# Moving a batch's loads behind another couple of a fused attention and max-out kernel, with four output buffers instead of three

## The chip, the cores and the metric

The kernel runs on one core of a Trainium2 chip. The metric is device time in microseconds (us), the median of several runs. The engines are TensorE (PE: matmuls, with its weight loads shown as PEld), VectorE (DVE), ScalarE (ACT), GpSimd (POOL) and SyncE (SP). PE multiplies into PSUM, DVE and ACT carry results from PSUM to SBUF, and POOL and SP do here little else than issue DMAs: POOL the loads from and the stores to memory (the software queue of the profile), SP the transposing DMAs from SBUF to SBUF (the hardware queue). Both queues feed the same 16 DMA engines.

## The reference

There are 8 batches of 3072 rows. For each batch a square score matrix is made from z alone, rectified and squared; it multiplies v, and the result is gated by u. All rows then go through a max-out layer.

```python
scores = (1.0 / S) * np.matmul(z, z.transpose(0, 2, 1))   # 8 x 3072 x 3072
attn = np.maximum(scores, 0.0) ** 2
x = u * np.matmul(attn, v)                                 # 8 x 3072 x 256
h1, h2 = x @ w1, x @ w2                                    # 24576 x 1024
out = np.maximum(h1, h2) @ w_out                           # 24576 x 256
```

The kernel uses that max(h1, h2) = relu(x(w1 - w2)) + x w2, so it keeps w1 - w2 and the product w2 w_out.

## The kernel before, in words

A batch has 24 tiles of 128 rows. Four tiles make a group (six to a batch), two groups make a couple (three to a batch); a couple is the unit of the main loop. The score matrix is cut into 6 by 6 blocks of 512 by 512. It is symmetric, so only the blocks on and above the diagonal are computed (`score_pair`: two matmuls into PSUM, line 204; a rectifying copy by ACT, line 217; squaring by DVE, lines 223 and 225). The blocks below the diagonal are mirrored by a transposing DMA on SP (`mirror`, line 246), and a diagonal block, of which only a triangle is computed in batches 1 to 7, is completed by three small transposes (line 228). Pairs of a coming couple or batch are computed between the steps of the present couple.

Batch 0 is special. Its groups 0 to 3 (couples (0,0) and (0,1)) are run as plain products, group by group, in the loop over `PLAIN` (line 262). Its last couple, (0,2), is run in the main loop as 96 steps of plain products over the blocks 2, 0, 1, 3, 5, 4 (line 835); in these steps 20 of the score pairs of batch 1 are computed, at steps 2, 6, 11, 16, 20 and on, up to 91. A pair needs the transposed z (tile `zT`) of the pieces it touches: piece 1 of batch 1 first at step 20, piece 2 first at step 58. From batch 1 on, each couple is computed with seven products of combined blocks instead of eight (`prepare`, the sums and differences S1 to S4 of blocks by DVE, line 300; of v by `combine_v`, lines 164 to 167).

The two matmuls of a step run in the two halves of PE's rows. Where a product passes from one half to the other, a `nop` on POOL stands between them (lines 844 to 849): POOL waits for the last matmul of the first half, and PE's first matmul in the second half waits for POOL. In couple (0,2) such a pair of relays stands every fourth step, and whatever is in POOL's queue ahead of a relay delays it.

The feed-forward part of a couple (`ff`, lines 435 to 476) runs one couple later: the 16 inner products `d_ps` go through ACT into the tiles `g_sb`, three ahead of their use, and the output of each group leaves in two halves (`leave`): ACT copies a PSUM bank into an `o_sb` buffer (line 475) and POOL issues the store (line 476). So a couple has four such copies, two after its first group and two at its end. `opool` has three buffers, so the fourth copy waits until the first store has landed. Couple (0,0)'s part runs between the plain groups and couple (0,2); the bank of its fourth copy is needed by the first step of couple (0,2).

The instructions stand in each engine's queue in the order in which the program calls them, and each queue is served in order. A load that has no buffer to wait for is issued as soon as POOL reaches it; `held=True` writes one element with DVE first, which makes the load wait for that DVE instruction.

Loads around the change: `load_v(1, 2)` at group 3, tile 18 (line 685, held), `load_u` for couple (0,2) in `loads_behind(1)` (line 710) and `load_v(1, 1)` just after (line 743) come before the feed-forward part of (0,0); each `load_v` is four DMAs of two tiles (128 KB). `load_v(1, 0)` comes in `loads_behind(2)`, at the end of couple (0,2). `turn_u` (line 180) transposes u on SP: for couple (0,2) at its steps 2 and 6 (line 813); the result is read by `gate` after the couple's last step. v of batch 1 is first read by `combine_v`, after couple (0,2).

Of the kernel before, what the change touches and what calls it, by code (L numbers as in the profile page):

```python
# [11 lines left out]
def kernel(  # L12
# [43 lines left out]
    rpool = ctx.enter_context(tc.tile_pool(name="rpool", bufs=3))  # L56
    hpool = ctx.enter_context(tc.tile_pool(name="hpool", bufs=5))
    xpool = ctx.enter_context(tc.tile_pool(name="xpool", bufs=4))
    gpool = ctx.enter_context(tc.tile_pool(name="gpool", bufs=8))
    opool = ctx.enter_context(tc.tile_pool(name="opool", bufs=3))  # L60
    mm_psum = ctx.enter_context(tc.tile_pool(name="mm_psum", bufs=4, space=bass.MemoryType.PSUM))
    acc_psum = ctx.enter_context(tc.tile_pool(name="acc_psum", bufs=1, space=bass.MemoryType.PSUM))

    def by_tile(x):
        return x.rearrange("(p t) d -> p t d", t=NT)
# [76 lines left out]
    def load_v(b, piece, lo=0, n=2 * G, held=False):  # L142
        if (b, piece) not in vp:
            vp[b, piece] = vpool.tile([P, 2 * G, D], bf16, name="v_sb")
        t = vp[b, piece]
        if held:
            nc.vector.memset(t[:, lo, 0:1], 0.0)
        step = 2 if b else n
        for at in range(lo, lo + n, step):
            nc.gpsimd.dma_start(  # L150
                out=t[:, ds(at, step), :], in_=by_tile(v[b])[:, ds(piece * 2 * G + at, step), :]
            )
# [21 lines left out]
    def load_u(b, g):  # L174
        un[b, g] = unat.tile([P, G, D], bf16, name="un")
        nc.gpsimd.dma_start(out=un[b, g], in_=by_tile(u[b])[:, ds(g * G, G), :])  # L176

    def turn_u(b, g):
        t = upool.tile([P, G, KD, P], bf16, name="uT")
        nc.sync.dma_start_transpose(  # L180
            t.rearrange("p a c r -> p (a c) r"), un[b, g].rearrange("p a d -> p (a d)")
        )
        uT[b, g] = t
# [318 lines left out]
    couples = [(b, c) for b in range(B) for c in range(NC)]  # L502
# [44 lines left out]
    def steps_of(i):  # L547
        tiles, both = range(NT), range(KD)
        head = edge(i - 1) if i else 0
        tail = NT - edge(i)  # L550
        steps = [(n, dc) for dc in both for n in tiles[:head]]
        steps += [(n, dc) for n in tiles[head:tail] for dc in both]
        return steps + [(n, dc) for dc in both for n in tiles[tail:]]

    def pair_slots(i):
        return (
            [1, 3] + list(range(6, 40, 4)),
            list(range(3, 41, 4)),
            list(range(3, 41, 4)),
            list(range(0, 44, 4)),  # L560
        )[i]

    def need(b, g, n):
        most = pair_at[b, g, 2 * g]
        for t in range(n + 1):
            if t // G >= g:
                most = max(most, pair_at[b, g, t // 2] + 1)
        return most

    with tc.manual_schedule():  # L570
# [17 lines left out]
        def new_acc():  # L588
            return {
                (half, dc): acc_tile(2 * half + dc) for half in range(2) for dc in range(KD)  # L590
            }
# [27 lines left out]
        for i in range(PLAIN):  # L619
            b, g = groups[i]  # L620
            if i:
                acc = new_acc()
            new, slots = {}, pair_slots(i)
            for slot, (n, dc) in enumerate(steps_of(i)):
                k = need(b, g, n)
                upto = max(k, min(done + 1, k + AHEAD)) if slot in slots else k
                while done < min(upto, len(pairs)):
                    emit_pair()
                if i == 0 and slot in (10, 22):
                    zT_pe(12 if slot == 10 else 20, 8 if slot == 10 else 4, "act")  # L630
                    if slot == 22:
                        for x in z_first:
                            x.release()
                attn_unit(b, g, n, acc, dc, n == 0, n == NT - 1)
                if n == NT - 1 and i < PLAIN - 1:
                    if i < 2:
                        new[dc] = drain_fast(acc, dc)
                    else:
                        new.update(drain(acc, [dc]))
                if dc:  # L640
                    continue
                if i in (1, 2) and n == 10:
                    for h in sums.values():
                        nc.vector.tensor_add(h[0], h[0], h[1])
                    sums = {k: h[0] for k, h in sums.items()}
                if i and n == 12:
                    xTs[groups[i - 1]], tasks = gate(*groups[i - 1], sums)
                    for task in tasks:
                        task()
                if i == 0 and n == 14:  # L650
                    turn_u(0, 0)
                if i + 1 < PLAIN:
                    if i and n == 1:
                        load_u(*groups[i + 1])
                    if n == (13 if i == 2 else 16):
                        turn_u(*groups[i + 1])
                if (i, n) in ((0, 20), (1, 10)):
                    w_in = ((w2_sb, moe_w2), (w1_sb, moe_w1)) if i == 0 else ((w_out_sb, moe_w_out),)
                    nc.vector.memset(w_in[0][0][:, 0, 0:1], 0.0)
                    for w_sb, w in w_in:  # L660
                        nc.gpsimd.dma_start(
                            out=w_sb, in_=w.rearrange("(c p) f -> p c f", p=P)
                        )
                if later and n % 4 == 0 and (i == 3 or i and n > 12):
                    later.sort(key=lambda block: (block[2] > 3, block[1], block[2]))
                    mirror(*later.pop(0))
                if i == 2 and n == 16:
                    nc.vector.tensor_sub(w15_sb, w1_sb, w2_sb)
                    w1.release()
                    for dc in range(KD):  # L670
                        tp = mm_psum.tile([P, KF, P], bf16, name="tpw", tag="mm")
                        for j in range(KF):
                            nc.tensor.transpose(
                                tp[:, j, :], w2_sb[:, dc, ts(j, P)], ident
                            )
                        nc.scalar.copy(w2T_sb[:, dc, :, :], tp)
                    w2.release()
                if (i, n) in ((1, 16), (2, 14)):
                    load_z(1, i - 1, held=True)
                if (i, n) in ((2, 8), (3, 10)):  # L680
                    turn_z(1, i - 2)
                if (i, n) == (3, 14):
                    load_z(1, 2, held=True)
                if (i, n) == (3, 18):
                    load_v(1, 2, held=True)
            if i == 2:
                for dc in range(KD):
                    ps = mm_psum.tile([P, D], fp32, name="w2o_ps", tag="mm")
                    for nb in range(KF):
                        nc.tensor.matmul(  # L690
                            ps,
                            w2T_sb[:, dc, nb, :],
                            w_out_sb[:, nb, :],
                            start=(nb == 0),
                            stop=(nb == KF - 1),
                        )
                    nc.scalar.copy(W2o_sb[:, dc, :], ps)
                w2T.release()
            sums = new
# [4 lines left out]
        def loads_behind(i):  # L704
            b, c = couples[i]
            if c == 2 and b + 1 < B:
                load_v(b + 1, 0)
            if i + 1 < len(couples):
                for q in range(2):
                    load_u(couples[i + 1][0], 2 * couples[i + 1][1] + q)  # L710
            if b and b + 1 < B and c < 2:
                load_z(b + 1, c + 1)
                load_v(b + 1, c + 1)
            if c == 2 and b + 2 < B:
                load_z(b + 2, 0)
# [23 lines left out]
        b, g = groups[PLAIN - 1]  # L739
        sums = drain(acc, range(KD))  # L740
        xTs[b, g], gates = gate(b, g, sums)
        loads_behind(PLAIN // 2 - 1)
        load_v(1, 1)
        forms, early, late = prepared(PLAIN // 2)
        second(PLAIN // 2 - 2, gates + [lambda: turn_z(1, 2)])

        for i in range(PLAIN // 2, len(couples)):
            b, c = couples[i]
            q1, q2 = 2 * c, 2 * c + 1
            target = min((b + 1) * per_batch + (-6, 8, 22)[c], len(pairs))  # L750
            steps, ends, marks, waits = steps_of_couple(
                b, c, forms, blocks=() if b else (2, 0, 1, 3, 5, 4)
# [37 lines left out]
            events = {}  # L790
# [19 lines left out]
                    events.setdefault(n, []).insert(0, do)  # L810
            if not b:
                events[len(steps)] = [after_plain]
            for n, do in ((2, lambda: turn_u(b, q1)), (6, lambda: turn_u(b, q2))):
                events.setdefault(n, []).append(do)
            if b and b + 1 < B:
                events.setdefault((30, 8, 8)[c], []).append(lambda: turn_z(b + 1, c))

# [78 lines left out]
```

## Time and profile before

| what | value |
|---|---|
| median of 3 runs | 933.38 us (931.15 to 936.52) |
| the profiled execution's own time | 935.3 us |
| its span | 933.4 us |
| PE busy | 908.8 us, 97% of the span |
| DVE, ACT, POOL busy | 684.2, 633.2, 140.9 us |
| hardware DMA queue (SP's transposes) | 91.14 MB, 64.0% of 16 engines' span |
| software DMA queue (POOL's loads and stores) | 53.62 MB, 30.6% |
| mean granted PE clock | 0.994 |

An engine's busy time is the union of its instructions. The view of waits says for how long an engine stood idle before a line, and which instruction ended it; the timeline lists instructions by start time, with the idle time before one in brackets, and can show SP's DMA issues (SPq), whose duration is the time that the issuing took SP. A window's row has the busy time of each engine in a stretch, the granted clock and the share of the DMA engines, which can be above 1 where transfers of two queues overlap. Stretches of couple (0,2): the plain groups end at 66.3 us, the feed-forward part of (0,0) ends at 82.0, the couple's steps end at 115.3, the feed-forward part of (0,1) ends at 131.3, where couple (1,0) begins.

### The profile page before, as it was taken

How to read it: one execution, taken by the hardware profiler on the slowest of the kernel's cores; microseconds unless marked ns; L12 is line 12 of the kernel's file. 1: busy time of each engine (PE TensorE's matmuls, PEld its weight loads, DVE VectorE, ACT ScalarE, POOL GpSimd, SP SyncE). 2: the span in 40 equal slices, each digit the busy share in tenths (PEclk: the TensorE clock that was granted, in tenths of full speed). 3: DMA queues.
4: the chain of work that ended last, by engine and by line, in shares of the span. 5: the costliest groups of instructions: out<-in, count | busy, mean ns of one | idle time of the engine just before them, and what ended most of it. 6: DMA issues, size and time to landing. Idle time of an engine off the chain costs nothing.

```text
span 933.4 us, 19582 instructions
## 1 busy us (share of the span) xinstructions
PE 908.8 (97%) x7490; PEld 530.5 (57%) x7538; DVE 684.2 (73%) x1043; ACT 633.2 (68%) x1219; POOL 140.9 (15%) x266
## 2 busy tenths in 40 slices
PE   8997999999999999999999999999999999999998
PEld 4454555664655656655556556566565564655655
DVE  6770569778787689776796868969689668795542
ACT  7794856767676777667767676766776767674543
POOL 3121111022011210220202102202021021000000
PEclk9998999999999999999999999999999999999999
DMA  9999899999998999989989899799998999986401
GB/s 186 166 195 178 135 221 154 195 113 208 168 127 176 173 164 162 166 150 187 150 151 187 136 179 182 123 190 139 173 188 126 192 139 189 160 124 128 87 24 68
DMA packets 391838, 146.01 MB, mean 156 GB/s; under 512 B 362944, under 2 KB 377664, under 8 KB 391744
## 3 DMA queue, kind: packets, MB, share of 16 engines
q1 hardware_dynamic: 359904, 91.14, 64.0%
q0 software_dynamic: 31840, 53.62, 30.6%
q8 instruction: 59, 0.97, 0.4%
q14 instruction: 35, 0.29, 0.1%
HBM read 59.77 MB, written 25.17 MB: 91 GB/s over the span
## 4 chain that ended last, share of the span: by engine, by line
PE 84%; DMA 5%; issue 5%; DVE 4%; ACT 1%; POOL 1%; ACTq 0%; DVEq 0%; POOLq 0%
PE acc L835 39%; PE acc L457 19%; PE d_ps L435 15%; PE s_ps L204 6%; PE acc L262 4%; DMA out_dram<-o_sb 3%; DVE blk L300 2%; DMA v_sb<-in_v_dram 1%; ACT r_sb L217 1%; DMA blk<-blk 1%; DVE blk L223 1%; POOL v_sb L150 0%; DVE blk L225 0%; DVE h_sb L771 0%; PE acc L597 0%
## 5 line engine op out<-in xcount | busy, mean ns | idle before, releaser
L835 PE MATMUL acc<-blk,v_sb 64*128 64x512 bf16 x2208 | 398.6, 379 | 9.3 <-ACT o_sb L475 5.8
L217 ACT ACTIVATE r_sb<-s_ps 128x512 bf16<-128x512 f32 (+3 forms) x664 | 330.3, 559 | 109.0 <-PE s_ps L204 62.5
L300 DVE TENSOR_TENSOR blk<-blk,blk 128x2048 bf16<-128x2048 bf16 x252 | 301.7, 1219 | 28.7 <-PE acc L835 15.2
L835 PE MATMUL acc<-blk,vt 64*128 64x512 bf16 x1512 | 311.9, 377 | 3.1 <-ACT o_sb L475 3.1
L448 ACT ACTIVATE g_sb<-d_ps 128x512 bf16<-128x512 f32 x376 | 217.9, 602 | 110.4 <-PE d_ps L435 89.9
L225 DVE TENSOR_TENSOR blk<-r_sb 128x1024 bf16<-128x1024 bf16 x251 | 170.2, 689 | 129.2 <-ACT r_sb L217 127.8
L835 PEld LDWEIGHTS <-v_sb 64*128 64x128 bf16 x2208 | 161.0, 95 | 132.8 <-issue 18.2
L457 PE MATMUL acc<-w_out_sb,g_sb 128*128 128x256 bf16 x1536 | 226.5, 273 | 0.0
L435 PE MATMUL d_ps<-xT,w_sb 128*128 128x512 bf16 x720 | 214.2, 379 | 2.6 <-issue 0.2
L457 PEld LDWEIGHTS <-g_sb 128*128 128x128 bf16 x1536 | 150.3, 98 | 84.0
L835 PEld LDWEIGHTS <-vt 64*128 64x128 bf16 x1512 | 123.3, 94 | 75.7 <-issue 10.0
L204 PE MATMUL s_ps<-zT 64*128 64x512 bf16 (+3 forms) x672 | 150.4, 358 | 2.1 <-DVE r_sb L215 0.5
L476 POOL DMA_DIRECT2D out_dram<-o_sb x92 | 49.9, 547 | 374.1 <-ACT o_sb L475 360.5
L435 PEld LDWEIGHTS <-w_sb 128*128 128x128 bf16 x768 | 73.3, 98 | 28.2 <-issue 9.8
L475 ACT COPY o_sb<-acc 128x512 f32<-128x512 f32 x96 | 52.3, 590 | 52.8 <-PE acc L457 31.4
L150 POOL DMA_DIRECT2D v_sb<-in_v_dram x90 | 48.5, 566 | 136.5 <-PE acc L835 105.5
L204 PEld LDWEIGHTS <-zT 64*128 64x128 bf16 x672 | 46.7, 95 | 38.7 <-issue 2.8
L223 DVE TENSOR_TENSOR blk<-r_sb 128x512 bf16<-128x512 bf16 (+3 forms) x170 | 46.2, 318 | 27.3 <-ACT r_sb L217 27.0
L771 DVE TENSOR_TENSOR h_sb<-h_sb,acc 128x512 f32<-128x512 f32 x84 | 55.3, 679 | 6.7 <-PE acc L835 6.7
L415 DVE SCALAR_TENSOR_TENSOR xT<-h_sb,uT 128x512 bf16<-128x512 f32 x96 | 59.9, 683 | 0.0
L176 POOL DMA_DIRECT2D un<-in_u_dram x48 | 26.2, 559 | 213.0 <-PE acc L835 167.1
L262 PE MATMUL acc<-blk,v_sb 64*128 64x512 bf16 x384 | 50.5, 376 | 1.9 <-DVE blk L225 1.1
(50 smaller groups left out, 274.1 us busy)
## 6 DMA issues: line engine op xcount, KB each, us to landing
out_dram<-o_sb POOLq DMA_DIRECT2D x92, 256.0 KB, 4.5
un<-in_u_dram POOLq DMA_DIRECT2D x48, 256.0 KB, 8.0
v_sb<-in_v_dram POOLq DMA_DIRECT2D x84, 128.0 KB, 8.3
blk<-blk SPq DMA_TRANSPOSE x246, 4.8
zn<-in_z_dram POOLq DMA_DIRECT2D x21, 128.0 KB, 8.5
v_sb<-in_v_dram POOLq DMA_DIRECT2D x6, 256.0 KB, 7.1
blk<-in_moe_w_dram POOLq DMA_DIRECT2D x2, 512.0 KB, 7.2
out_dram<-o_sb SPq DMA_DIRECT2D x4, 256.0 KB, 2.1
```

Source lines behind the costliest of these rows:

```text
L204: nc.tensor.matmul(s_ps[h][:, lo[h] :], zT[rows, z_at(b, blk * G + tiles[h]), :], zT[rows, q + lo[h] // P : q + G, :].rearrange("p t c -> ...
L217: nc.scalar.activation(o, s, AF.Relu)
L223: nc.vector.tensor_mul(a[:, tiles[h], lo[h] :], o, o)
L225: nc.vector.tensor_mul(a[:, k : k + 2, :], r, r)
L262: nc.tensor.matmul(a.out(acc[half, dc]), v_at(b, t, dc)[rows], a.moving(rows, j), start=first, stop=last,)
L300: op(*((by_key(x) if mixed else x.ap) for x in blocks))
L415: lambda dc=dc: nc.vector.scalar_tensor_tensor(out=x[:, dc, :].rearrange("p (t r) -> p t r", r=P), in0=hs[dc].rearrange("p (t r) -> p t r" ...
L435: nc.tensor.matmul(d_ps, w15_sb[:, kc, ts(nb, P)], xs[q][:, kc, :], start=(kc == 0), stop=(kc == KD - 1),)
L448: nc.scalar.activation(g_sb[q, nb], d_ps, AF.Relu)
L457: nc.tensor.matmul(o_ps[key][:, t % 2, :], x[:, ts(t, P)], w, start=first, stop=ends and t % 2 == 1 and n == len(weights) - 1,)
L771: nc.vector.tensor_add(out, a, b_)
L835: mm = nc.tensor.matmul(a.out(acc[name]), w()[rows], a.moving(rows, j), start=first, stop=left[name] == 0, skip_group_check=True,)
```

## The change

`load_v(1, 2)` and `load_v(1, 1)` are removed from their places, with the DVE write that held the first. In couple (0,2) eight loads of two tiles each are put at steps 12, 19, 26, 33, 40, 47, 54 and 61: the four of piece 2, then the four of piece 1. The two loads of u for couple (0,2) move from ahead of the feed-forward part of (0,0) to the couple's steps 0 and 4, and their transposes from steps 2 and 6 to 40 and 46. `opool` has four buffers, `gpool` seven.

On POOL, the four stores of (0,0) now come ahead of these ten loads, and the ten loads stand between the relays of the couple. On SP, the two transposes of u move behind the six small transposes of two diagonal blocks and the mirrors of the blocks (1,2) and (1,3) of batch 1. PE and ACT keep their order; DVE has one memset of one element less.

```diff
-    gpool = ctx.enter_context(tc.tile_pool(name="gpool", bufs=8))
-    opool = ctx.enter_context(tc.tile_pool(name="opool", bufs=3))
+    gpool = ctx.enter_context(tc.tile_pool(name="gpool", bufs=7))
+    opool = ctx.enter_context(tc.tile_pool(name="opool", bufs=4))
...
-                if (i, n) == (3, 18):
-                    load_v(1, 2, held=True)
...
-            if i + 1 < len(couples):
+            if i + 1 < len(couples) and (b, c) != (0, 1):
                 for q in range(2):
                     load_u(couples[i + 1][0], 2 * couples[i + 1][1] + q)
...
         loads_behind(PLAIN // 2 - 1)
-        load_v(1, 1)
...
-            for n, do in ((2, lambda: turn_u(b, q1)), (6, lambda: turn_u(b, q2))):
+            for n, do in (
+                (2 if b else 40, lambda: turn_u(b, q1)),
+                (6 if b else 46, lambda: turn_u(b, q2)),
+            ):
                 events.setdefault(n, []).append(do)
+            if not b:
+                events.setdefault(0, []).append(lambda: load_u(b, q1))
+                events.setdefault(4, []).append(lambda: load_u(b, q2))
+                for n in range(8):
+                    events.setdefault(12 + 7 * n, []).append(
+                        lambda n=n: load_v(1, 2 - n // 4, 2 * (n % 4), 2)
+                    )
```

## The prediction

> **What bounds the kernel.** I read the busy times first. PE fills the span, so a change can only pay where PE stands still or runs at a lower clock.
>
> ```profile
> PE 908.8 (97%) x7490; PEld 530.5 (57%) x7538; DVE 684.2 (73%) x1043; ACT 633.2 (68%) x1219; POOL 140.9 (15%) x266
> ```
>
> Next the view of waits, for PE and for the engine that PE waits on. Columns: total us, times, longest.
>
> ```profile
> ACT o_sb L475 <- DMA out_dram<-o_sb: 16.9, 7, 5.0
> ...
> PE acc L835 <- ACT o_sb L475: 8.9, 4, 5.8
> ...
> PE acc L835 <- DVE blk L300: 2.2, 2, 1.1
> ```
>
> PE's largest idle groups behind the couples' matmuls are ACT's output copy, itself often waiting for a store to land, and DVE's block sums. The timeline of PE places them; the number in brackets is the idle time.
>
> ```profile
> 82.02 0.39 PE L835 MATMUL acc<-blk,v_sb 64*128 64x512 bf16 x1
> 88.18 1.01 PE L835 MATMUL acc<-blk,v_sb 64*128 64x512 bf16 x3 [5.77 <-ACT o_sb L475]
> ...
> 135.37 0.59 PE L835 MATMUL acc<-blk,v_sb 64*128 64x512 bf16 x3 [1.07 <-DVE blk L300]
> 137.77 0.58 PE L835 MATMUL acc<-blk,v_sb 64*128 64x512 bf16 x1 [1.14 <-DVE blk L300]
> ...
> 251.20 0.37 PE L835 MATMUL acc<-blk,vt 64*128 64x512 bf16 x1 [1.29 <-ACT o_sb L475]
> ```
>
> The other two of the four stand at 474.51 (1.10) and 809.74 (0.73). The chain of waits through the first one:
>
> ```profile
> 76.16 11.28 DMA out_dram<-o_sb
> 87.54 0.59 ACT o_sb L475
> 88.18 1.01 PE acc L835 x3
> ```
>
> The first store took 11.3 us to land, against a median of 4.5 over the kernel. What it shared the DMA engines with is seen in the issues of POOL, then SP, before it:
>
> ```profile
> 65.70 2.12 POOL L150 DMA_DIRECT2D v_sb<-in_v_dram  x4 [0.91 <-DVE v_sb L147]
> 67.78 1.10 POOL L176 DMA_DIRECT2D un<-in_u_dram  x2
> 68.82 1.13 POOL L150 DMA_DIRECT2D v_sb<-in_v_dram  x2
> ```
>
> ```profile
> 61.08 4.86 SPq L246 DMA_TRANSPOSE blk<-blk  x2
> 66.03 9.33 SPq L246 DMA_TRANSPOSE blk<-blk  x1
> 75.41 10.33 SPq L246 DMA_TRANSPOSE blk<-blk  x1
> 85.84 4.78 SPq L246 DMA_TRANSPOSE blk<-blk  x1
> 90.72 1.25 SPq L134 DMA_TRANSPOSE zT<-zd  x1
> ```
>
> A mirror takes SP 2.4 us before the loads and 9 to 10 with them: loads, stores and mirrors share full engines, and SP falls behind. The windows show the price on PE's clock (PEclk, third from the right) and DMA engines that are free later:
>
> ```profile
> 86.00:90.00 4.00, 1.82 (x10) 1.03 (x11) 0.12 (x1) 1.33 (x3) 0.54 (x1) 0.54 1.21 224
> 90.00:94.00 4.00, 4.00 (x27) 2.30 (x25) 1.14 (x4) 1.34 (x5) 0.00 (x0) 0.61 1.24 283
> ...
> 106.00:110.00 4.00, 4.00 (x40) 2.03 (x38) 2.20 (x4) 3.58 (x8) 0.00 (x0) 1.00 0.24 49
> ```
>
> **The change, part by part.** All is summed against the profiled span, 933.4 us, which is the median of the runs (933.38); that execution's own time was 935.3, 1.9 above.
>
> A, the wait at 82 to 88. With four buffers the fourth copy has one of its own. ACT was idle 5.05 us before it, so it starts at 82.49, ends at 83.07, and PE restarts at 83.13 instead of 88.18. Saved: 5.05 us; 0.7 us of idle time stays, since the bank must still be copied.
>
> B, the clock behind it. The granted clock is half from 86.29 to 93.12 in the trace. PE works in 4.94 us of that (from 88.18), and does half: 2.47 us lost. With 0.7 us idle the clock has no reason to fall: the 1.29 us stop at 251 left it at 1.00. Saved: 2.47 us.
>
> C, the wait at 135 to 138. PE waits for block differences by DVE, and DVE's chain had stood 4.53 us for a mirror that SP issued at 127.63 and that landed at 134.0: SP's backlog from 66 on, carried forward. The two stops make 2.21 us, and the clock is half again from 137.49 to 140.90, 3.13 us of it worked: 1.56 us. Will the mirror come in time? Without loads the three mirrors from 66.03 take about 2.5 us each (61.08 to 66.03 held two), so the transpose of z issued at 90.72 goes at about 74 to 76, and SP is idle until DVE finishes the first diagonal block at step 12. Couple (0,2) then runs 83.1 to 107.8 (24.7 us at full clock). SP has from about 87: six small transposes at 1.28 (7.7), two mirrors, u's two transposes (3.4 before), two mirrors, then the one in question. Mirrors cost 2.5 alone and 3.7 to 7.3 in the stretch 110 to 127 before, with loads beside them; I take 4 for the first two and the 7.3 and 4.1 of before for the next two, where v's piece 0 and u fall: 87 + 7.7 + 8 + 3.4 + 11.4 = 117.5, landing 6.4 later as before: 123.9. DVE wants it at 129.57 - 7.52 = 122.05, and PE waits only if the last of DVE's three differences behind the mirror (3.7 us of work) is late for the matmul at 137.77, which without the two stops and with A and B stands at 137.77 - 2.21 - 7.52 = 128.0: the mirror may land until 124.3. Between ends: 2.5 a mirror throughout gives 114.5 for the landing and all 3.77 us saved; 10 for the first two gives 136 and a PE stop of some 12, which needs loads as dense as those of 66 to 73 (ten in 7 us), while here ten are spread over 16. The middle is nearest; I take C in full, 3.77 us, and keep 0 and worse for the range.
>
> D, the later stops. 251.20, 474.51 and 809.74 follow the same fourth copy: ACT idled 3.38 us before that at 250.56, 3.18 at 473.88, and at 809.10 the store issued at 799.95 had landed at 809.00. With a fourth buffer: 1.29 + 1.10 + 0.73 = 3.12 us. The other waits of ACT for stores (210, 361, 622, 694) held no PE stop over 0.2 us: nothing.
>
> E, the ten loads between relays. A load takes POOL 0.53 to 0.67 us (v, 90 of them). Relays come in pairs about 1.08 us apart (94.53 and 95.00, then 95.45 and 95.66, and so on); at most one load stands between two pairs and starts just after the earlier. So 0.67 fits, cost 0; no row has a load there, so the other end is ten times 0.67, 6.7 us, if nothing of it were covered. Each load also waits for the DMA eight places before it. That is a store of (0,0) for the third to sixth of v and a load of u for the last two: stores landed in 4.4 to 11.3 us, u in 11.8 to 12.6 at the worst, against 13 us from u's issue (84) to the seventh load of v (97). Cost 0, with half a microsecond in hand.
>
> [...]
>
> F, the rest. Seven tiles of g: only three are made ahead of their use, so nothing waits; eight or seven make no difference. The removed memset is 0.06 us of DVE, idle there for 20 us. u's transposes land near 107 by the sum above; the gates that read them ran after 137 (130 now): 20 us of cover. v's last part, issued at 99.8, lands by 113 at worst (13.2 in the stretch of ten loads), by 107 at its median of 8.3; DVE wants piece 1 from 109.7, so 3 us of DVE's chain are at stake in the worst case.
>
> Sum: 5.05 + 2.47 + 3.77 + 3.12 = 14.4, and 933.4 - 14.4 = 919.0.
>
> **The rivals.**
>
> 1, C does not come: the mirrors of batch 1 stay late because v's parts now run beside them. For it: SP is at 100% of its time from 35 to 140. Against it: the free engines of 102 to 110. A, B, D alone: 10.6 us, 922.8; every microsecond that the mirror lands later than before's own lag adds one, so 925 at 2 us. It decides from a landing at 124.3 on, by the sum in C only 0.4 us away.
>
> 2, the first stop is replaced. Couple (0,2) now starts 5 us earlier, and its pair at step 20 (88.2) needs the transposed z that landed at 94.2 before. If SP is not ahead, PE waits 6.0 us there, and a fall of the clock may follow: 919 + 6 to 8.5 = 925 to 927.5. It decides if the three mirrors from 66.03 take over 6.3 us each; 2.5 without loads speaks against it.
>
> 3, the DMA congestion only moves, and A, B and C all go to later waits: D alone, 930.3, same.
>
> 4, slower: POOL holds PE. Each load stands ahead of relays. If a load took POOL, or its wait, 2.5 us (1.08 of spacing plus 1.44), ten would eat the 14.4; from about 3 us on it is slower than before by the bound below: 933.4 + 5 = 938. Longest load before: 0.673.
>
> **How the numbers follow.** Half a per cent (4.7 us) is about what a measurement of this kernel can tell from no change. Chances: forecast 0.55, its own range 916.3 to 921.7 (half of the spread of the runs before, 2.7); rival 1 0.22; rival 2 0.10; rival 3 0.06; rival 4 0.07. The range goes from 916.3 to rival 2's middle, 926.5. Faster (below 928.7): 0.87; same 0.06; slower 0.07.
>
> [...]
>
> **What will show it.** A: no idle time over 1 us before the first L835 near 83, no ACT wait for stores anywhere. B and C: the granted clock at 1.00 from 5 us to the end of the work. SP's transpose of z near 75, not 90. D: no L835 stop behind L475 after batch 1. E: relays (L844) in pairs at 1.08 us with loads between. The prediction falls if PE stops in couple (0,2) behind POOL or DMA, or if DVE's chain before couple (1,0) still waits for a mirror or now for v.

## The result and the profile after

The changed kernel took 930.68 us (median of 20 runs, 919.1 to 941.92), the kernel before, timed beside it, 939.41 us (20 runs, 931.15 to 958.65). The ratio is 0.9891, with a 95% interval from 0.9856 to 0.9926; timed once more later it was 0.9928 (0.9886 to 0.9971). The ratios leave out the slow executions of both kernels, so they differ a little from the quotients of the medians (0.9907 here). So the change makes the kernel about 1% faster, where 1.54% (14.4 of 933.4 us) had been forecast, and the time is above the range. Part of the distance is the starting point: the three runs that the forecast started from (933.38) lie at the low end of what the kernel before does.

The profiled execution (934.33 us, the fourth longest of the twenty) has a span of 932.6 us, 0.8 below the one before it. Its view of waits for PE:

```profile
PE acc L842 <- DVE blk L300: 9.2, 3, 7.4
PE acc L842 <- DVE h_sb L768: 3.3, 2, 1.6
PE s_ps L204 <- DMA zT<-zd: 1.9, 2, 1.2
...
PE acc L842 <- ACT o_sb L475: 0.6, 1, 0.6
```

ACT's output copy has gone from 8.9 to 0.6 us, and DVE's block sums have grown from 2.2 to 9.2. (The couples' matmul is line 842 now, the relay 851.) The timeline of PE has both places:

```profile
82.10 0.39 PE L842 MATMUL acc<-blk,v_sb 64*128 64x512 bf16 x1
83.11 0.59 PE L842 MATMUL acc<-blk,v_sb 64*128 64x512 bf16 x3 [0.62 <-ACT o_sb L475]
...
125.80 1.02 PE L842 MATMUL acc<-blk,v_sb 64*128 64x512 bf16 x7
134.24 1.01 PE L842 MATMUL acc<-blk,v_sb 64*128 64x512 bf16 x3 [7.42 <-DVE blk L300]
```

The 5.77 us stop at 82 is 0.62 us long, as forecast. But couple (1,0), which starts some 7.5 us earlier, stands for 7.42 us at nearly the same moment as before (134.24 against 135.37). The chain of waits leads through one transfer:

```profile
111.52 21.35 DMA blk<-blk
132.87 0.03 issue
```

This is the mirror of block (1,4) of batch 1. The timelines of SP and of DVE show it from both ends:

```profile
104.48 3.10 SPq L246 DMA_TRANSPOSE blk<-blk  x1
107.69 3.72 SPq L246 DMA_TRANSPOSE blk<-blk  x1
111.52 12.49 SPq L246 DMA_TRANSPOSE blk<-blk  x1
```

```profile
119.57 0.43 DVE L165 TENSOR_TENSOR v_sb<-v_sb 128x512 bf16<-128x512 bf16 x1 [6.71 <-DMA v_sb<-in_v_dram]
...
122.30 3.61 DVE L300 TENSOR_TENSOR blk<-blk,blk 128x2048 bf16<-128x2048 bf16 x3
132.96 3.62 DVE L300 TENSOR_TENSOR blk<-blk,blk 128x2048 bf16<-128x2048 bf16 x3 [7.05 <-DMA blk<-blk]
```

In the kernel before, SP had issued the same mirror later, and DVE had waited less for it:

```profile
127.63 3.33 SPq L246 DMA_TRANSPOSE blk<-blk  x1
...
134.09 3.62 DVE L300 TENSOR_TENSOR blk<-blk,blk 128x2048 bf16<-128x2048 bf16 x3 [4.53 <-DMA blk<-blk]
```

SP now reached it at 111.52, 16 us earlier than before, but needed 12.5 us to issue it, and it landed 21.35 us after its issue began (6.4 before). Beside it stood the loads from the end of couple (0,2):

```profile
106.69 2.12 POOL L150 DMA_DIRECT2D v_sb<-in_v_dram  x4 [6.88 <-PE s_ps L204]
108.77 1.10 POOL L176 DMA_DIRECT2D un<-in_u_dram  x2
109.81 0.59 POOL L126 DMA_DIRECT2D zn<-in_z_dram  x1
```

DVE waited for both: 6.71 us for v's piece 0, then 7.05 us for the mirror. Without the second wait its sums would have gone on at 125.9 (122.30 + 3.61) instead of 132.96, so the mirror is what held PE. PE's granted clock fell to 0.50 within the stop and stayed there behind it, as the windows show (third from the right):

```profile
131.00:133.00 2.00, 0.00 (x0) 0.00 (x0) 0.04 (x1) 0.00 (x0) 0.00 (x0) 0.50 1.29 178
133.00:137.00 4.00, 2.68 (x12) 0.91 (x13) 3.97 (x4) 0.98 (x2) 0.00 (x0) 0.50 1.21 201
```

A landmark says what is gained and given back in these two executions. The feed-forward part of (0,1) begins at 107.92 instead of 115.41: 7.49 us gained. The next one, behind couple (1,0), begins at 156.24 instead of 157.37: 1.13 us are left. From there to the end it is 776.3 us against 776.1.

### The profile page after: what moved, and what is told of

Read it like the earlier page. It is cut to its first block, busy times and chain, and to the rows that moved or that the text cites. A ratio compares the mean times of both kernels' runs of the same rounds, so it can differ in the third digit from the quotient of the medians.

```text
span 932.6 us, 19607 instructions
## 1 busy us (share of the span) xinstructions
PE 906.0 (97%) x7490; PEld 524.2 (56%) x7538; DVE 684.3 (73%) x1042; ACT 634.5 (68%) x1219; POOL 140.8 (15%) x266
## 4 chain that ended last, share of the span: by engine, by line
PE 89%; DMA 5%; DVE 4%; issue 1%; ACT 1%; POOL 0%; ACTq 0%; DVEq 0%; POOLq 0%
PE acc L842 41%; PE acc L457 21%; PE d_ps L435 16%; PE s_ps L204 6%; PE acc L262 4%; DMA blk<-blk 2%; DMA v_sb<-in_v_dram 2%; DVE blk L300 2%; DMA zT<-zd 1%; DVE blk L225 1%; DVE xT L415 0%; ACT r_sb L217 0%; DVE blk L223 0%; PE w2o_ps L688 0%; POOL v_sb L150 0%
## 5 line engine op out<-in xcount | busy, mean ns | idle before, releaser
L225 DVE TENSOR_TENSOR blk<-r_sb 128x1024 bf16<-128x1024 bf16 x251 | 170.3, 690 | 129.4 <-ACT r_sb L217 128.2
L204 PE MATMUL s_ps<-zT 64*128 64x512 bf16 (+3 forms) x672 | 140.8, 358 | 2.9 <-DMA zT<-zd 1.9
L204 PEld LDWEIGHTS <-zT 64*128 64x128 bf16 x672 | 42.5, 94 | 40.3 <-DMA zT<-zd 2.8
```

The lines of the kernel that those rows point to most:

```text
L204: nc.tensor.matmul(s_ps[h][:, lo[h] :], zT[rows, z_at(b, blk * G + tiles[h]), :], zT[rows, q + lo[h] // P : q + G, :].rearrange("p t c -> ...
L225: nc.vector.tensor_mul(a[:, k : k + 2, :], r, r)
```

## The experiments

Ratios are to the kernel before, timed in the same set. The profiles are of one execution each.

**1. The pool sizes alone.** The loads stay where the kernel before has them.

```diff
 (the kernel before)
-    gpool = ctx.enter_context(tc.tile_pool(name="gpool", bufs=8))
-    opool = ctx.enter_context(tc.tile_pool(name="opool", bufs=3))
+    gpool = ctx.enter_context(tc.tile_pool(name="gpool", bufs=7))
+    opool = ctx.enter_context(tc.tile_pool(name="opool", bufs=4))
```

> The kernel before with the two pool sizes alone (four output buffers, seven tiles of g); the loads stay where they were. Theory (the moved loads free SP, the fourth buffer only removes the copy's wait): PE restarts at 83.1 instead of 88.2, but the transposed z of batch 1's second piece still lands near 94, so PE stops about 5 to 6 us behind zT in couple (0,2); what remains is the 3.1 us of the later stops, 928 to 931 against 933.4, ratio 0.995 to 0.998. Rival (the buffer is the whole gain): no stop over 1 us between 83 and 108, and the ratio of the full change, 0.989.

Measured: 931.1 us (10 runs, 925.52 to 951.77), ratio 0.9918 (0.9876 to 0.9960). PE restarts at 83.10, and is then stopped twice in couple (0,2):

```profile
86.23 0.82 PE L835 MATMUL acc<-blk,v_sb 64*128 64x512 bf16 x6 [0.98 <-POOLq L844]
100.91 0.61 PE L204 MATMUL s_ps<-zT 64*128 64x512 bf16 x2 [11.64 <-DMA zT<-zd]
```

The stop behind the transposed z is there, twice the size expected: SP issued that transpose only at 97.13, after two mirrors that took it 17.32 and 8.89 us. The first stop, 0.98 us, is behind a relay on POOL. Ahead of it in POOL's queue stood the stores of (0,0), which in the author's reading waited for the loads of u eight places before them, as loads of v did in experiment 10 (3.60 and 0.99 us). So in this execution (938.38 us, the third longest of its ten) the fourth buffer's gain at 82 was lost again within 20 us, which is what the moved loads are there to prevent. Yet the median does not show it: with the pools alone the kernel is as fast as with the whole change, within the interval. How often the stop is as long as here is not known from one profile.

**2. The moves alone.** The changed kernel with three output buffers and eight tiles of g.

```diff
 (the changed kernel)
-    gpool = ctx.enter_context(tc.tile_pool(name="gpool", bufs=7))
-    opool = ctx.enter_context(tc.tile_pool(name="opool", bufs=4))
+    gpool = ctx.enter_context(tc.tile_pool(name="gpool", bufs=8))
+    opool = ctx.enter_context(tc.tile_pool(name="opool", bufs=3))
```

> The changed kernel with three output buffers and eight tiles of g, so the moved loads alone. Theory: the first store lands near 80, before the fourth copy at 82.5 asks for its buffer, so the stop at 83 stays under 1 us as in the full change; the stops behind the output copy in later batches come back (251, 474, 810 in the kernel before: 3.1 us). Ratio 0.991 to 0.993. Rival (without the buffer the move is worth nothing): ACT waits for a store of 3 us or more near 83, ratio 0.998 or above.

Measured: 936.26 us (10 runs, 926.12 to 953.57), ratio 1.0009 (0.9935 to 1.0082). The profiled execution agrees with the theory: 0.62 us idle at 83.48 and no other stop in couple (0,2), so the moved loads alone free the first store. The later stops are back, and longer than in the kernel before:

```profile
464.63 0.37 PE L842 MATMUL acc<-blk,vt 64*128 64x512 bf16 x1 [0.88 <-ACT o_sb L475]
```

with 1.52 us at 540.40 and 2.61 us at 802.26: 5.0 us, and a fall of the clock behind the last. The stop in front of couple (1,0) is only 0.91 and 1.14 us here, though the loads stand where the changed kernel has them: the mirror of (1,4) was issued at 117.46 and landed at 126.73. But the ratio is above the expected 0.991 to 0.993, and most of the ten runs are well above the profiled one (its span is 927.6). Without the fourth buffer the moved loads show no gain that this timing could tell; why the median is that far from the profile is open.

**3. Next batch's u and z out of the burst.** The loads of u for couple (1,0) go to its steps 0 and 4, their transposes to 40 and 46, the load of z of batch 2 to step 8 and its turning to step 52. The burst at the end of (0,2) is then v's piece 0 alone.

```diff
-            if i + 1 < len(couples) and (b, c) != (0, 1):
+            if i + 1 < len(couples) and (b, c) not in ((0, 1), (0, 2)):
...
-            if c == 2 and b + 2 < B:
+            if c == 2 and b and b + 2 < B:
                 load_z(b + 2, 0)
...
+            late_u = i in (2, 3)
...
-                (2 if b else 40, lambda: turn_u(b, q1)),
-                (6 if b else 46, lambda: turn_u(b, q2)),
+                (40 if late_u else 2, lambda: turn_u(b, q1)),
+                (46 if late_u else 6, lambda: turn_u(b, q2)),
...
-            if not b:
+            if late_u:
                 events.setdefault(0, []).append(lambda: load_u(b, q1))
                 events.setdefault(4, []).append(lambda: load_u(b, q2))
+            if i == 3:
+                events.setdefault(8, []).append(lambda: load_z(2, 0))
+            if not b:
...
-                events.setdefault((30, 8, 8)[c], []).append(lambda: turn_z(b + 1, c))
+                events.setdefault((52 if i == 3 else 30, 8, 8)[c], []).append(lambda: turn_z(b + 1, c))
```

> The changed kernel, with the two loads of u for couple (1,0) moved from the end of couple (0,2) to steps 0 and 4 of (1,0), their transposes to steps 40 and 46, the load of z of batch 2 to step 8 and its transpose to step 52. Theory (the 7.4 us stop at 134 comes from the mirrors of batch 1 sharing the DMA engines with the burst of loads at 107 to 110): 0.625 MB less in the burst, the mirror that DVE waits for lands 4 us or more earlier than 132.9, PE's stop falls to under 3.5 us, and the kernel is 4 to 8 us faster than the changed one. Rival (the eight parts of v at 87 to 100 have made SP late): mirror and stop stay within 1.5 us of where they are.

Measured: 928.96 us (4 runs), ratio 0.9890 (0.9780 to 1.0000), too few runs to tell. The mirror landed at 118.7 instead of 132.9, and PE has no stop at all between 84 and 160. Later in couple (1,0), to which the loads have gone, it has two, 1.57 us at 175.03 behind DVE's block sums and 1.64 at 178.84, and the clock is at half for 3.4 us. DVE's six sums run without a break:

```profile
117.87 7.27 DVE L300 TENSOR_TENSOR blk<-blk,blk 128x2048 bf16<-128x2048 bf16 x6
```

It was timed again in a later set:

> The kernel of e3_late_u, timed again with more rounds, since four executions did not tell it from the changed kernel. If the smaller burst is what matters: ratio 0.982 to 0.988 and a stop under 3 us at 128 to 136. If it was one lucky execution: 0.989 to 0.993 and a stop of 4 us or more.

Measured: 921.72 us (6 runs), ratio 0.9790 (0.9745 to 0.9835), better than expected; the mirror landed at 126.6, again without a stop at its place (0.66 us at 143.97 is another one), though PE waited 1.94 us for zT at 101.61. So the smaller burst takes the stop away, in both profiles, while the spread parts of v, which are in all these kernels, stay where they were.

**4. The transposes of u back at steps 2 and 6.**

```diff
 (the changed kernel)
-                (2 if b else 40, lambda: turn_u(b, q1)),
-                (6 if b else 46, lambda: turn_u(b, q2)),
+                (2, lambda: turn_u(b, q1)),
+                (6, lambda: turn_u(b, q2)),
```

> The changed kernel with the transposes of u back at steps 2 and 6 of couple (0,2); the loads of u stay at steps 0 and 4. Theory (SP is served in order): SP stands at the first of them until u has landed near 90.5 and 91.5, so the six small transposes begin near 93 instead of 84.8, the mirrors behind them follow some 4 us later, and the stop at 134 grows by 0 to 5 us; 0 to 5 us slower than the changed kernel. Rival (the moved transposes made the mirrors late): the mirror lands earlier and the stop is shorter.

Measured: 928.1 us (10 runs, 921.6 to 933.29), ratio 0.9883 (0.9831 to 0.9935): the same as the changed kernel within the interval. SP did stand until u had landed, and the small transposes ran from 94.5 instead of 84.8. The mirror of (1,4) was issued at 120.98 (111.52 in the changed kernel) but landed at 130.55 (132.87), the stop is 5.12 us (7.42). So being issued 9 us later did not make the mirror land later, which points to the DMA engines and not to SP's time; two single executions can't show more. Where the transposes of u stand makes no difference that this timing could tell.

**5. The two kernels profiled again.**

> The kernel before, unchanged, profiled once more, to see which of its stops belong to the kernel and which to the one execution. Theory (stops that end on a transfer differ from execution to execution by several us, because the times to landing do; stops that end on an engine don't): the stop at 82 to 88 lies between 3 and 9 us, the one at 134 between 0 and 8, the stops behind the output copy after batch 1 add up to between 2 and 10 instead of 3.1; the stops before 66 us agree to 0.3 us. Rival (the profile read for the forecast is typical): every stop over 1 us is found again within 1 us of its size.

Measured, the kernel before: span 936.0. The stop at 88 is 4.54 us, at 135 to 138 it is 1.01 and 1.14, behind the output copy 2.13 (476.40) and 1.39 (812.32). So the stop at 82 and the sum of the later ones are found again within 1.3 us. Of the later ones, the two at 474 and 810 are found again, larger, and the one at 251 is gone. The stops before 66 us agree, but for one of 0.70 at 50. The truth lies between the two expectations.

> The changed kernel, unchanged, profiled again and timed beside the two variants below. Theory (the mirror before couple (1,0) is late by a different amount in each execution): no stop over 1 us between 83 and 108, the stop near 128 to 134 anywhere between 1 and 8 us. Rival (the change always trades the stop at 82 for one of 7 us at 134): 6.5 to 8.5 us again.

Measured, the changed kernel: 933.83 us (12 runs), span of the profiled one 932.0. PE stops 2.67 us behind zT at 101.46, and

```profile
141.21 1.01 PE L842 MATMUL acc<-blk,v_sb 64*128 64x512 bf16 x3 [9.35 <-DVE blk L300]
```

The stop is larger than the theory's 1 to 8 and the rival's 6.5 to 8.5. Here SP reached the mirror of (1,4) late:

```profile
127.06 6.87 SPq L246 DMA_TRANSPOSE blk<-blk  x1
```

It landed at 139.84, and DVE waited 12.23 us for it. In all, the changed kernel and its variant with the transposes of u back stood 7.4, 9.4 and 5.1 us here.

**6. The transpose of z earlier, the loads at their old places.**

```diff
 (the kernel before, with the pool sizes)
-                if (i, n) in ((2, 8), (3, 10)):
+                if (i, n) in ((2, 8), (3, 0)):
                     turn_z(1, i - 2)
```

> The kernel before with the two pool sizes, the loads at their old places, and the transpose of z of batch 1's second piece put two mirrors earlier on SP (at group 3, tile 0 instead of 10). Theory (with the loads left where they were, PE waits at step 20 for that transpose, which stands behind three slow mirrors): the stop of 11.6 us before 101 falls to under 6, what is left ends on zT at step 58 or on a mirror; 2 to 8 us faster than with the pools alone. Rival (PE waits for the DMA engines as such, so that another transfer is late instead): a stop of 9 us or more stays in couple (0,2).

Measured: 931.93 us (10 runs), ratio 0.9930 (0.9890 to 0.9969), no faster than the pools alone. The profile is of the longest of the ten (942.78 us). The stop behind zT is down to 1.61 us (90.67) and 2.38 (103.49), as the theory has it; but 12.79 us then follow at 147.08, behind the same mirror in front of couple (1,0). Here the rival is right in substance: what PE gains in (0,2) it waits for in (1,0).

**7. No burst at all.** As experiment 3, with v's piece 0 as four loads at steps 68, 74, 80 and 86 of couple (0,2).

```diff
 (on top of experiment 3)
-            if c == 2 and b + 1 < B:
+            if c == 2 and b and b + 1 < B:
                 load_v(b + 1, 0)
...
+                for n in range(4):
+                    events.setdefault(68 + 6 * n, []).append(
+                        lambda n=n: load_v(1, 0, 2 * n, 2)
+                    )
```

> The changed kernel with u and z of the next batch moved into couple (1,0) as in e3_late_u, and v's piece 0 of batch 1 as four loads at steps 68, 74, 80 and 86 of couple (0,2) instead of at its end, so that no burst of loads is left at 107 to 110. Theory (the burst beside the mirrors makes the stop at 134): the mirror that DVE waits for lands before 126, the stop is under 2 us, and the kernel is 3 to 8 us faster than the changed one, ratio to the kernel before 0.981 to 0.987. Rival (mirrors and any loads together are too much for the DMA engines, wherever the loads stand): a stop over 4 us near 128 to 134, and no difference from the changed kernel beyond the interval.

Measured: 925.72 us (12 runs), ratio 0.9871 (0.9833 to 0.9909), against 0.9928 of the changed kernel in the same set; the intervals overlap. The stops are 2.73 and 1.14 us, with the clock at half for 3.4 us behind them, and the mirror landed at 128.2, so both lie between theory and rival: loads that are spread over 18 us still slow the mirrors beside them (that of (1,3), issued at 99.73, landed at 114.6, 14.9 us later; the four issued from 55 to 66 in the kernel before, with two loads among them, landed after 5.6 at their median). Compared with experiment 3, spreading is no better than a burst of four.

**8. The mirror ahead of the burst.** Same work and same transfers as the changed kernel; block (1,4) of batch 1 is computed third instead of fifth, and so mirrored third.

```diff
 (the changed kernel)
+            if (b, c) == (1, 0):
+                for g, blk in ((1, 2), (1, 3), (1, 4), (0, 2), (0, 3), (1, 5), (0, 4), (0, 5)):
+                    add_block(b, g, blk)
+                continue
             for o in range(c + 1, NC):
                 for g, k in ((1, 0), (1, 1), (0, 0), (0, 1)):
                     add_block(b, 2 * c + g, 2 * o + k)
```

> The changed kernel with the blocks of batch 1 computed in another order in couple (0,2): block (1,4) third instead of fifth, so that its mirror, for which DVE waits before it may overwrite the block, is issued third on SP and not fifth, ahead of the burst of loads. Same work, same transfers. Theory (the stop at 134 is this mirror's lateness): it lands before 118, the stop of 7.4 and 9.4 us falls to under 2.5 (what is left is DVE's own chain behind v's piece 0), the clock does not fall there, 5 to 11 us faster than the changed kernel, ratio to the kernel before 0.980 to 0.987. Rival (SP and DMA are late as a whole, so the next transfer takes its place): a stop of 5 us or more at 128 to 136 stays, or one moves to couple (1,0) or (1,1), and the ratio stays at 0.989 to 0.993.

Measured: 922.98 us (6 runs, 916.78 to 927.89), ratio 0.9818 (0.9767 to 0.9870); span of the profiled execution 914.9. The mirror was issued at 104.85 and landed at 115.1. PE's waits, all over 0.6 us, are:

```profile
PE acc L846 <- DVE h_sb L772: 1.5, 1, 1.5
PE acc L601 <- DVE blk L578: 1.2, 1, 1.2
PE acc L262 <- DVE blk L225: 1.1, 3, 0.5
PE acc L846 <- ACT o_sb L475: 0.6, 1, 0.6
```

The 9.2 us behind DVE's block sums are gone, nothing took their place, and the clock stays at full until the last microseconds. DVE waited for v's piece 0 as before, but for no mirror:

```profile
116.25 0.43 DVE L165 TENSOR_TENSOR v_sb<-v_sb 128x512 bf16<-128x512 bf16 x1 [2.36 <-DMA v_sb<-in_v_dram]
...
118.98 7.27 DVE L300 TENSOR_TENSOR blk<-blk,blk 128x2048 bf16<-128x2048 bf16 x6
```

This shows the cause: with every load where the change puts it, the place of one mirror in the order is what decides. Up to the feed-forward part behind couple (1,0), the profile gains 9.77 us on that of the changed kernel (146.47 against 156.24), about what the stop and the clock behind it had cost; all six executions are below the changed kernel's median. The order asks for one thing earlier: piece 2 of the transposed z is needed at step 39 instead of 58. It landed at 84.44 here, but at 101.41 in the second profile of the changed kernel, and there a pair at step 39 would have had to wait for it.

**9. Both.** Experiment 8 on top of experiment 3.

> The changed kernel with this order of blocks and with u and z of the next batch loaded inside couple (1,0) (as in e3_late_u). Theory: no stop over 2 us from 83 to 140; 0 to 3 us faster than with the order of blocks alone; ratio 0.978 to 0.986. Rival: as slow as the changed kernel, 0.989 to 0.993.

Measured: 922.13 us (6 runs), ratio 0.9816 (0.9762 to 0.9869), span 916.0, no stop over 0.7 us from 83 to 160. Not to be told from experiment 8 or the second timing of experiment 3. By the ratios each of the three beats the kernel before, and also the changed kernel as timed the second time (0.9886 to 0.9971); with its first timing (0.9856 to 0.9926) the intervals of experiments 8 and 9 still overlap a little.

**10. All eight parts at one step.** The price of loads that stand together among the relays.

```diff
 (the changed kernel)
-                    events.setdefault(12 + 7 * n, []).append(
+                    events.setdefault(12, []).append(
```

> The changed kernel with all eight parts of v at step 12 of couple (0,2), so that eight loads of some 0.53 us stand together ahead of the relays of step 15 on POOL. Theory (a relay waits for what is ahead of it in POOL's queue): POOL is busy for 4.3 us from 86.9, the relay comes some 3 us late, and PE stops 2.5 to 4 us behind POOL near 88. Rival (relays pass, or have more slack than a step or two): no stop over 0.5 us there.

Measured in a single execution: 935.01 us, span 933.2. POOL's and PE's timelines:

```profile
86.93 3.17 POOL L150 DMA_DIRECT2D v_sb<-in_v_dram  x6 [1.36 <-PE acc L842]
93.69 0.53 POOL L150 DMA_DIRECT2D v_sb<-in_v_dram  x1 [3.60 <-DMA un<-in_u_dram]
95.22 0.53 POOL L150 DMA_DIRECT2D v_sb<-in_v_dram  x1 [0.99 <-DMA un<-in_u_dram]
```

```profile
95.38 2.31 PE L842 MATMUL acc<-blk,v_sb 64*128 64x512 bf16 x10 [6.97 <-POOLq L851]
```

The mechanism is real and dearer than thought: six loads took 3.17 us, and the seventh and eighth waited for the loads of u eight places before them, 3.60 and 0.99 us. The relays behind them came late, and PE stood for 6.97 us. Spread over the steps, in the changed kernel, the same loads stop no relay: u, issued at 83.93 and 84.97, had landed 6.4 us later, and the seventh load came at 97.13. This execution shows one thing more: with couple (0,2) held up, SP issued the mirror of (1,4) at 113.40, ahead of the burst, which began at 116.52. It landed at 120.51, and PE had no stop behind DVE's block sums.

## Why the prediction was right or wrong

**A, the wait at 82: right.** 0.62 us are left in both profiles of the changed kernel, 0.7 had been forecast, and the part behind couple (0,2) begins 7.49 us earlier (7.52 forecast for A and B). Experiments 1 and 2 show that either half of the change does it: with four buffers the copy doesn't wait (PE restarts at 83.10), and with the moved loads the first store lands before the copy asks (0.62 us idle at 83.48).

**B, the clock behind it: right.** It stays at full speed from 83 to 108 where no other stop follows (granted clock 1.00 in the first profile, 0.86 in the kernel before); in the second profile a 2.67 us stop behind zT brought it down for 3.4 us. That stop is not the forecast's second rival, which was the pair of step 20 behind SP's backlog (it came in experiment 1, 11.64 us). It is the pair of step 58, for piece 2 of z, which SP issued at 85.00 and which landed 16.41 us later, beside the loads that the change put there. The sum had no term for it. It came in two of the eight profiled executions that have both the moved loads and the fourth buffer, spread over the steps (2.67 us, and 1.94 in experiment 3 timed again).

**C, the wait before couple (1,0): wrong, and this is the step that failed.** In the first profile the sum was on the safe side with SP (mirror reached at 117.5 by the sum, 111.52 measured); its last term was mis-sized: "landing 6.4 later as before". It landed 21.35 us later, 15 more than the sum had. The 6.4 came from a stretch in which the loads of the burst had landed when that mirror was issued (z at 126.4, the mirror at 127.63). With the whole couple 7.5 us earlier and SP 16 us earlier, the same mirror stood in the middle of the burst. In the second profile the terms before it were short as well: the six small transposes took SP 13.0 us where the sum had 7.7, and the mirror just before took it 9.17, so that it reached (1,4) at 127.06, and the mirror landed 12.78 later. In the four profiles with the loads moved, the whole burst and this order (experiments 2 and 4 are the others; in experiment 10 the mirror was ahead of the burst) the term of 6.4 is 9.27 to 21.35 us, and the stop 2.05, 5.12, 7.42 and 9.35. So in the first profile the 3.77 us to be saved became a loss: 7.42 us, and 6.8 us at half clock, of which PE worked 3.28, so 1.64 lost: 9.1 us against 3.8 before. In its outcome that is the first rival, with its growing stop, whose deciding point ("only 0.4 us away") the text had named and given 0.22. In its cause it is so only in part: the rival blamed the parts of v that now run in couple (0,2), and they may have slowed the small transposes of the second profile; but experiments 3 and 8 have these parts too, and there the stop goes when the burst at the couple's end is smaller or comes behind the mirror.

**D, the later stops: right in kind, a little small.** None is left in any profile with four buffers. In executions with three they made 3.1, 3.5 and 5.0 us: two of them, near 475 and 810 in the kernel before, came in all three profiles, the third at 251 or 540 or not at all. The clock fell behind the 2.61 us of experiment 2; behind the 1.29, 1.10 and 0.73 us of the kernel before it stayed at 1.00. The rest of the span from the part behind couple (1,0) on is 776.1, 777.3 and 777.6 us with three buffers, and 768.5 to 776.3, mean 772.1, in the eleven profiles with four. By these means it is some 5 us, not 3.1; single executions differ by more than that, and in the first profile of the changed kernel (776.3) other stops and a fall of the clock (3.4 us at half from 485.7) took up the gain.

**E, the loads among the relays: right as a cost, and right as a danger.** In the change's spacing no stop ends on POOL: PE has no wait behind it in the first profile of the changed kernel, and none of 0.6 us or more in the second. Each v load in couple (0,2) took POOL 0.53 us in the first, with DVE at work for 8.70 of the 16 us from 84 to 100. What the fourth rival named (something ahead of a relay) stopped PE for 0.98 us in experiment 1 and 6.97 in experiment 10, in experiment 10 by the issuing (3.17 us) and by the wait for earlier transfers (3.60 and 0.99 us), in experiment 1, in the author's reading, by such a wait of the stores.

**Short stops and the clock.** The prediction read the clock's cost from single rows: none behind the stop of 1.29 us at 251, half clock behind those of 1.07 and 1.14 us at 135 to 138. The runs have both outcomes for stops of nearly one size. In the second profile of the kernel before, one gap of 1.64 us at 149.60 was followed by 3.4 us at half clock from 149.77; a gap of 1.47 us in experiment 8 was not. The pair in front of couple (1,0) was 1.01 and 1.14 us in the second profile of the kernel before, and the first matmul behind it took 0.37 us, against 0.58 at half clock in the first profile. In the first profile of the changed kernel a gap of 1.64 us at 485.51 was followed by 3.4 us at half clock and one of the same length at 148.81 was not (granted clock 1.00 from 146 to 153), so the length of a gap alone didn't decide in these runs.

**The sum.** A, B and D make 10.6 us, which gives the ratio 0.9886 and is what was measured (0.9891). That agreement is partly luck: C's loss of some 5 us stands against a D that is larger than forecast and against a kernel before whose usual execution is slower than the one that was read. The timings also don't show that the moved loads add anything to the fourth buffer: the pool sizes alone have 0.9918, the whole change 0.9891 and 0.9928, the moves alone 1.0009. Three readings in the prediction are slightly off without bearing on the sum: POOL's stores landed in 2.3 to 11.3 us, not 4.4 to 11.3; the four mirrors of 110 to 127 took SP 2.2 to 7.3, not 3.7 to 7.3; and the middle of the second rival is 926.25, not 926.5.

## What to carry to other kernels

When work ahead of a saturated queue is made faster, the transfers behind it move too, as here a mirror that was issued 16 us earlier and landed 21.35 us after its issue instead of 6.4: place each of them anew against the loads that it will now meet, rather than carry its old time to landing along. Ask of a transfer that many are waiting for whether it can be issued before the burst; here that was a change of order which showed no cost in six executions and by the ratios was worth nearly as much again as the change itself. And what a store or a mirror takes in one profiled execution is one draw (the mirror of (1,4) took 9.27 to 21.35 us in four profiles, and the stop behind the first store was 5.77 and 4.54 in two of the kernel before): more profiles of a kernel tell which of its stops are its own, as here those near 475 and 810 and not the one at 251.

## What the runs showed of the hardware that was not expected

Transposes and loads that share the DMA engines slowed each other here by more than a split of the bandwidth. Mirrors alone, from 61 to 66 in the kernel before, moved 234 GB/s at a DMA share of 1.14 (so a share above 1 doesn't take two queues). In the changed kernel's stretch from 107 to 133, with loads and stores, the engines moved 3.66 MB at 141 GB/s though their share was 1.27; in the stretch 110 to 134 of the kernel before, with the same loads and stores, it was 4.54 MB at 189 GB/s, share 1.18. The difference is in the transposes, 1.82 MB against 2.80. A mirror of 0.5 MB took SP some 2.4 us in that stretch from 61 to 66; with loads beside it up to 12.5 in the changed kernel and 17.3 in experiment 1. What makes the mixed stretch that slow, and why it differs between executions, was not found.
